# Shorter channel loads, a byte limit on transfers in flight, and a new hand-written order, in a fused RWKV-5 and SwiGLU kernel

## The chip, the cores and the metric

The kernel runs on one core of a Trainium2 chip. A time is the time of one execution on the device, in microseconds (us). Three executions of the kernel before took 593.34, 594.98 and 597.05 us; the median is 594.98 us. One more execution was profiled.

## What is computed

The reference first runs a linear attention with a decaying state (RWKV-5), on 4 batches, 8 heads, 768 tokens and 48 channels a head, and then a SwiGLU layer on the 3072 tokens of 384 features:

```python
for t in range(S):
    kt, vt, rt = (k[:, :, t], v[:, :, t], r[:, :, t])
    cur = np.einsum('bhd,bhe->bhde', u[None] * kt, vt)
    y[:, :, t] = np.einsum('bhd,bhde->bhe', rt, state + cur)
    state = w[None, :, :, None] * state + np.einsum('bhd,bhe->bhde', kt, vt)
...
xn = x / rms * rms_g                  # rms over the 384 features
g = xn @ w_gate                       # 384 x 1536
silu = g * (1.0 / (1.0 + np.exp(-g)))
return ((silu * (xn @ w_val)) @ w_out).astype(np.float32)
```

`w_gate`, `w_val` and `w_out` arrive as 64-bit floats. Everything else is 32-bit.

## The kernel before

**Chunks.** The 768 tokens are cut into 12 chunks `s` of L = 64; a chunk of all 4 batches is NT = 256 tokens. For each chunk SyncE (SP) loads three tiles: `CH` (r and k with channels on the partitions), `TOK` (r and k with tokens on the partitions) and `V`. There is one buffer of each, so a load waits for the last reader of the chunk before. `CH` has 128 partitions: two groups of 64, each with 48 rows of channels and 16 rows of zeros.

**Mixing.** `mixing(s)` does a chunk of attention. For chunks 0 and 1 it multiplies k by u (`ku`, ScalarE), makes the diagonal scores from it (PE products `E`), scales r and k by powers of w (`R`, `K`: VectorE, for half of chunk 0 GpSimd), makes the scores (PE products `A`), puts them behind a mask into `MT` (`d` and `m`, VectorE), and makes the outputs from `MT`, `V` and the state `ST` (PE products `Y`). ScalarE takes `sq` (squares) and `yT` (outputs) out of PSUM; the mean square goes through PE (`r`), VectorE (`ms`), GpSimd (`pow`), VectorE (`inv`, `diag`) and PE (`spread`); `x` is the scaled result, `xb` a copy with the partition halves exchanged. The new state needs `KH` (VectorE, from `TOK` and the table `wk`) and the PE products `U`, which also read `V`. Some outputs are moved to other partitions by two small DMAs (`move`).

**SwiGLU.** The layer of chunks 0 and 1 is done product by product (`cell`, `project`): a product is 12 matmul records. The chunks from 2 on are done in pairs, with seven products in place of eight on sums of weights and of tokens (`group`, `second_layer`). Three PSUM tiles, `bank_a`, `bank_b` and `bank_c`, take the products in turn; `at` is a fourth, for the attention.

**Weights.** Each piece of a weight is loaded as 64-bit words (`raw`, 6 buffers; 384 words a partition for the first six pieces, then 576), and made 32-bit by three engines: `bits` (VectorE, two instructions), `ulp` (ScalarE) and their sum (GpSimd) into `wa`, `wb` or `wo`. In the text "wa0.1" is the second piece of `wa_0`. Later the weights are loaded once more in 36 pieces (`look`), which ScalarE examines (`check`); the result decides whether another version of the whole computation runs. It does not run here.

**Order.** All this is recorded as 1536 steps in a `Plan`. `ORDER` is a list, written out by hand, that says in which order the steps are given; each engine does its own in that order. At the start the numbers mean: 5, 6 loads of k (first and second half of the batches), 7, 8 of r, 9 of `TOK`, 10 of `V`; 11, 16, 21, 26, 31, 36 loads of wa0.0, wb0.0, wa0.1, wb0.1, wa0.2, wb0.2 (each followed by its `ulp`, two `bits` and sum); 41 and 42 `ku`, 43 and 44 `E`, 45 to 48 `R` and `K`, 49 and 50 `A`, 51 and 58 `d`, 52 and 59 `m`, 53 and 60 `Y`, 67 `ms`, 71 `spread`; 100, 101 and 102 the loads of `CH`, `TOK` and `V` for chunk 1.

**Gaps.** Where the plan sees TensorE idle it puts matmuls of a tile of ones with itself (`warm`), one letter of `unused` naming the bank for each gap. They compute nothing.

**Transfers.** Loads on SP go through `InOrder.at_most`: each waits until the fourth load before it has landed (`IN_FLIGHT` = 4). The loads of `look`, the moves and the stores are not counted. SP works in order, so what stands behind a waiting load waits too.

```python
FIRST, IN_FLIGHT = 2, 4
def load_chan(s):
    sp.at_most(IN_FLIGHT, lambda: sp.dma_start(out=CH, in_=chan[s]))
```

Of the kernel before, what the change touches and what calls it, by code (L numbers as in the profile page):

```python
# [49 lines left out]
P = 128  # L50
# [22 lines left out]
def feature_order():  # L73
# [10 lines left out]
    0, 6, 8, 42, 44, 5, 4, 7, 21, 11, 10, 41, 43, 16, 1, 2, 3, 45, 46, 47, 76, 12, 51, 48, 49, 52, 53, 55, 31, 36, 26,  # L84
    13, 14, 58, 50, 59, 15, 54, 17, 22, 60, 62, 65, 66, 100, 18, 19, 23, 24, 113, 9, 108, 103, 20, 67, 68, 83, 56, 27,
    61, 84, 63, 64, 57, 25, 69, 70, 38, 33, 39, 28, 71, 72, 124, 77, 86, 78, 126, 90, 29, 34, 118, 193, 85, 79, 87,
    30, 123, 80, 133, 32, 127, 125, 102, 81, 195, 82, 105, 106, 104, 37, 200, 128, 134, 35, 40, 107, 91, 131, 129,
    109, 114, 95, 130, 132, 92, 135, 119, 73, 110, 136, 96, 137, 155, 115, 111, 120, 116, 205, 210, 121, 139, 140, 97,
    138, 101, 93, 75, 74, 279, 112, 117, 141, 142, 143, 156, 150, 151, 157, 122, 98, 196, 163, 159, 160, 144, 197,
    198, 149, 145, 161, 206, 201, 164, 146, 199, 191, 274, 192, 284, 88, 152, 158, 162, 147, 148, 167, 218, 207, 202,  # L90
    165, 168, 169, 166, 203, 212, 213, 171, 172, 215, 170, 216, 208, 175, 176, 204, 209, 179, 180, 211, 177, 173, 217,
    174, 178, 183, 187, 89, 181, 182, 276, 219, 277, 153, 227, 275, 184, 188, 281, 194, 289, 280, 222, 282, 321, 311,
    306, 185, 225, 189, 247, 248, 249, 186, 214, 154, 190, 99, 278, 283, 251, 252, 255, 285, 250, 253, 254, 220, 256,
    257, 94, 238, 259, 263, 260, 264, 291, 286, 287, 288, 258, 267, 313, 308, 292, 314, 307, 224, 290, 228, 221, 271,
    316, 293, 261, 312, 268, 317, 265, 269, 223, 226, 309, 229, 331, 326, 336, 272, 266, 270, 262, 310, 315, 298, 302,
    294, 295, 242, 230, 322, 233, 234, 328, 355, 352, 318, 323, 299, 303, 296, 231, 300, 304, 297, 232, 353, 356, 235,
    236, 243, 327, 346, 319, 324, 305, 301, 329, 237, 244, 341, 273, 386, 390, 391, 387, 246, 354, 358, 245, 357, 320,
    325, 330, 332, 359, 362, 388, 392, 342, 333, 338, 334, 343, 344, 335, 339, 347, 337, 340, 345, 361, 364, 365, 348,
    360, 389, 375, 407, 349, 380, 363, 383, 381, 239, 393, 384, 500, 350, 366, 406, 394, 395, 351, 368, 369, 416, 437,
    367, 396, 241, 370, 501, 371, 382, 405, 404, 502, 398, 372, 399, 400, 373, 504, 503, 397, 438, 507, 509, 240, 374,  # L100
    376, 408, 378, 512, 377, 401, 402, 445, 409, 410, 385, 403, 413, 439, 446, 456, 457, 417, 441, 440, 447, 411, 442,
    462, 443, 444, 448, 451, 449, 463, 450, 464, 452, 453, 455, 454, 506, 458, 460, 465, 505, 459, 470, 467, 471, 466,
    468, 472, 508, 469, 473, 414, 415, 418, 590, 461, 422, 481, 474, 412, 476, 482, 510, 477, 478, 475, 483, 518, 591,
    513, 480, 484, 489, 485, 511, 479, 486, 490, 491, 487, 514, 488, 628, 492, 627, 519, 515, 520, 525, 493, 495, 624,
    526, 527, 496, 625, 497, 494, 521, 499, 528, 533, 523, 522, 530, 534, 419, 420, 423, 421, 424, 428, 524, 516, 517,
    425, 636, 529, 535, 498, 531, 544, 532, 626, 536, 634, 539, 598, 537, 545, 629, 540, 647, 541, 633, 538, 546, 543,
    547, 552, 635, 549, 548, 542, 550, 551, 630, 553, 631, 555, 554, 558, 632, 556, 563, 559, 560, 562, 565, 564, 557,
    567, 637, 426, 427, 429, 430, 566, 651, 568, 561, 571, 569, 570, 574, 582, 584, 575, 572, 573, 599, 577, 576, 578,
    638, 579, 434, 431, 583, 600, 595, 596, 601, 639, 581, 580, 592, 606, 585, 589, 593, 611, 432, 433, 588, 435, 586,
    602, 603, 587, 597, 436, 607, 642, 612, 643, 700, 640, 594, 747, 644, 701, 608, 615, 645, 756, 641, 652, 609, 610,  # L110
    646, 748, 614, 648, 649, 749, 616, 613, 617, 619, 618, 681, 744, 745, 650, 605, 653, 654, 621, 604, 682, 620, 657,
    746, 622, 683, 623, 660, 826, 689, 656, 684, 655, 685, 754, 690, 757, 753, 751, 691, 686, 706, 687, 688, 692, 695,
    693, 707, 708, 696, 697, 699, 709, 694, 702, 658, 703, 704, 714, 711, 698, 712, 715, 659, 661, 750, 662, 710, 663,
    705, 716, 717, 713, 725, 718, 755, 762, 719, 666, 720, 726, 827, 752, 727, 721, 723, 758, 722, 724, 728, 863, 733,
    860, 730, 664, 665, 763, 734, 729, 731, 732, 667, 669, 735, 736, 759, 760, 739, 864, 737, 769, 740, 771, 861, 741,
    770, 764, 765, 865, 743, 862, 772, 777, 866, 738, 766, 767, 670, 778, 668, 671, 774, 742, 773, 775, 780, 675, 779,
    776, 783, 834, 781, 867, 873, 782, 788, 784, 785, 790, 789, 835, 787, 791, 796, 793, 792, 786, 869, 797, 798, 794,
    795, 799, 802, 883, 800, 870, 676, 807, 803, 804, 806, 809, 808, 810, 801, 815, 812, 672, 673, 674, 677, 816, 768,
    761, 811, 805, 678, 888, 813, 818, 814, 821, 819, 817, 836, 831, 832, 871, 822, 823, 820, 872, 868, 825, 824, 828,
    829, 833, 874, 837, 843, 838, 679, 680, 844, 875, 839, 830, 878, 879, 847, 876, 841, 980, 981, 846, 877, 887, 880,  # L120
    842, 881, 845, 848, 851, 882, 884, 889, 886, 885, 984, 850, 891, 852, 890, 853, 919, 855, 849, 917, 918, 983, 920,
    982, 854, 856, 857, 990, 840, 858, 922, 921, 923, 924, 893, 859, 925, 892, 896, 931, 936, 926, 937, 927, 932, 933,
    928, 942, 929, 935, 944, 943, 945, 986, 938, 985, 939, 894, 930, 940, 934, 993, 895, 947, 950, 998, 987, 951, 946,
    948, 899, 1063, 941, 953, 952, 949, 954, 956, 961, 957, 1096, 958, 963, 962, 960, 964, 988, 992, 955, 965, 966,
    989, 969, 959, 967, 968, 972, 1097, 900, 897, 970, 898, 991, 975, 973, 976, 994, 901, 971, 1098, 905, 1001, 977,
    974, 979, 978, 999, 1005, 1000, 1007, 1006, 1003, 1013, 1008, 1002, 1010, 1009, 1011, 1012, 995, 1102, 1014, 1015,
    1070, 1016, 1019, 1017, 1105, 902, 903, 904, 908, 1062, 1024, 1020, 1021, 1119, 1023, 1026, 1025, 1027, 1018,
    1106, 1028, 1029, 1032, 1022, 1030, 1031, 1035, 1033, 1100, 1034, 1038, 1036, 1043, 1039, 906, 1103, 1040, 1045,
    1044, 1124, 1004, 1037, 909, 907, 911, 996, 1047, 1042, 1046, 1099, 1048, 1041, 1049, 1051, 1071, 1050, 1101,
    1109, 910, 1123, 1054, 1052, 1108, 1104, 1107, 997, 914, 1057, 1055, 1216, 1056, 1110, 1060, 1053, 1058, 1059,  # L130
    1061, 1064, 1072, 1111, 912, 1065, 1114, 1115, 1067, 1068, 1073, 1078, 1074, 1075, 1083, 1172, 1173, 913, 1069,
    1112, 1217, 1066, 1219, 915, 916, 1113, 1116, 1084, 1079, 1117, 1080, 1118, 1120, 1218, 1121, 1122, 1082, 1125,
    1126, 1087, 1229, 1076, 1088, 1086, 1089, 1091, 1085, 1155, 1127, 1153, 1154, 1077, 1128, 1156, 1093, 1094, 1158,
    1157, 1159, 1160, 1220, 1092, 1090, 1081, 1095, 1161, 1167, 1228, 1223, 1162, 1225, 1163, 1164, 1168, 1129, 1169,
    1226, 1165, 1171, 1174, 1221, 1234, 1177, 1299, 1178, 1132, 1180, 1298, 1166, 1222, 1179, 1175, 1176, 1186, 1170,
    1181, 1224, 1227, 1182, 1332, 1183, 1187, 1184, 1185, 1230, 1232, 1130, 1131, 1333, 1188, 1189, 1192, 1190, 1197,
    1193, 1135, 1335, 1194, 1199, 1198, 1235, 1191, 1196, 1200, 1205, 1195, 1202, 1203, 1133, 1134, 1206, 1201, 1138,
    1207, 1208, 1204, 1334, 1211, 1209, 1241, 1212, 1336, 1344, 1231, 1236, 1136, 1213, 1243, 1242, 1210, 1345, 1337,
    1237, 1215, 1244, 1214, 1249, 1238, 1239, 1246, 1245, 1250, 1251, 1247, 1248, 1137, 1139, 1140, 1144, 1252, 1255,
    1253, 1338, 1341, 1254, 1260, 1256, 1257, 1306, 1259, 1262, 1261, 1307, 1263, 1268, 1265, 1258, 1266, 1269, 1264,  # L140
# [18 lines left out]
class InOrder:  # L159


    def __init__(self, tc, engine):
        self.tc, self.engine, self.flying = tc, engine, []

    def at_most(self, n, give):


        made = give()
# [79 lines left out]
def fast(ctx, tc, chan, tok, vpad, wka, wkb, wot, cols, u_row, out, bad):  # L248
# [124 lines left out]
    def load_chan(s):  # L373
        sp.at_most(IN_FLIGHT, lambda: sp.dma_start(out=CH, in_=chan[s]))
# [1477 lines left out]
```

## Time and profile before

| what | value |
|---|---|
| median of three executions | 594.98 us |
| profiled execution | 594.46 us |
| its span, first to last instruction | 592.7 us |
| outside the span | 1.8 us |
| TensorE (PE) busy | 582.0 us, 98% of the span |
| VectorE (DVE), ScalarE (ACT), GpSimd (POOL) busy | 70%, 50%, 7% |
| moved by DMA | 62.99 MB, mean 106 GB/s |
| mean granted TensorE clock | 0.998 |

Busy time is the share of the span in which an engine has an instruction running. PE's matmuls are pipelined and their ends are modelled, so their records overlap: a product of 12 records shows 1.46 us long, but the next starts 1.30 us later. The warm matmuls count as busy. Line 179 is a helper through which nearly all instructions are given, so work is told apart by tiles. "A <- B" in a list of waits means that A was idle until B ended, and "issue" that the profile shows no cause. SPq is SyncE's queue of DMA issues.

### The profile page before, as it was taken

How to read it: one execution, taken by the hardware profiler on the slowest of the kernel's cores; microseconds unless marked ns; L12 is line 12 of the kernel's file. 1: busy time of each engine (PE TensorE's matmuls, PEld its weight loads, DVE VectorE, ACT ScalarE, POOL GpSimd, SP SyncE). 2: the span in 40 equal slices, each digit the busy share in tenths (PEclk: the TensorE clock that was granted, in tenths of full speed). 3: DMA queues.
4: the chain of work that ended last, by engine and by line, in shares of the span. 5: the costliest groups of instructions: out<-in, count | busy, mean ns of one | idle time of the engine just before them, and what ended most of it. 6: DMA issues, size and time to landing. Idle time of an engine off the chain costs nothing.

```text
span 592.7 us, 16598 instructions
## 1 busy us (share of the span) xinstructions
PE 582.0 (98%) x7280; PEld 520.5 (88%) x7280; DVE 415.3 (70%) x622; ACT 293.8 (50%) x713; POOL 41.9 (7%) x40
## 2 busy tenths in 40 slices
PE   8999999999999999999999999999999999999996
PEld 7888887668888998888999889999889999988995
DVE  7888769595786977776795667795777585455641
ACT  5864458364366654564462474584365473124100
POOL 2443234100000000000000000000000000000000
PEclk9999999999999999999999999999999999999999
DMA  7975463412613123512222415301531200301002
GB/s 268 337 254 232 167 239 90 146 34 55 213 55 116 55 75 103 198 36 97 82 92 67 143 58 187 133 8 40 165 119 62 69 29 17 92 2 54 2 4 55
DMA packets 22768, 62.99 MB, mean 106 GB/s; under 512 B 2944, under 2 KB 9760, under 8 KB 21280
## 3 DMA queue, kind: packets, MB, share of 16 engines
q1 hardware_dynamic: 21920, 61.36, 30.8%
q8 instruction: 58, 0.95, 0.7%
q10 hardware_dynamic: 768, 0.49, 0.3%
q14 instruction: 22, 0.18, 0.1%
HBM read 56.04 MB, written 4.72 MB: 103 GB/s over the span
## 4 chain that ended last, share of the span: by engine, by line
PE 95%; DMA 2%; DVE 1%; issue 1%; ACT 0%; SPq 0%; POOL 0%; DVEq 0%
PE bank_b L179 33%; PE bank_c L179 27%; PE bank_a L179 27%; PE at L179 8%; DMA V<-in_vpad_dram 1%; DMA chan<-in_chan_dram 1%; DVE ms L179 0%; DVE KH L179 0%; ACT ku L179 0%; SPq L179 0%; ACT wk L179 0%; POOL ms L179 0%; ACT diag L179 0%; DVE rows_out L179 0%; DVE diag L179 0%
## 5 line engine op out<-in xcount | busy, mean ns | idle before, releaser
L179 DVE TENSOR_TENSOR gv<-bank_b,m 128x512 f32<-128x512 f32 x90 | 62.1, 690 | 63.5 <-PE bank_b L179 59.2
L179 ACT ACTIVATE gv<-gv 128x512 f32<-128x512 f32 (+1 forms) x60 | 30.8, 522 | 74.9 <-DVE gv L179 74.7
L179 DVE TENSOR_TENSOR gv<-bank_c,gv 128x512 f32<-128x512 f32 x60 | 41.4, 690 | 21.7 <-PE bank_c L179 21.2
L179 PE MATMUL bank_b<-xa,wa 64*128 64x256 f32 x444 | 55.3, 379 | 0.0
L179 PEld LDWEIGHTS bank_b<-xa,wa 64*128 64x128 f32 x444 | 43.2, 187 | 5.0 <-issue 0.7
L179 PE MATMUL bank_a<-xb,wb 64*128 64x256 f32 x372 | 46.5, 379 | 0.0
L179 PE MATMUL bank_a<-xa,wa 64*128 64x256 f32 x372 | 46.0, 378 | 0.0
L179 PE MATMUL bank_b<-t,s 64*128 64x256 f32 x360 | 45.2, 379 | 0.6 <-issue 0.6
L179 PE MATMUL bank_a<-wo,h 128*128 128x192 f32 x264 | 45.2, 327 | 0.0
L179 ACT ACTIVATE MT<-dmask,du 128x64 f32<-128x64 f32 x160 | 41.8, 336 | 6.1 <-DVE du L179 6.0
L179 PE MATMUL bank_b<-t,wb 64*128 64x256 f32 x360 | 44.6, 378 | 0.0
L179 PE MATMUL bank_c<-t,s 64*128 64x256 f32 x360 | 44.4, 376 | 0.0
L179 PE MATMUL bank_c<-xb,s 64*128 64x256 f32 x360 | 44.2, 376 | 0.0
L179 PEld LDWEIGHTS bank_a<-wo,h 128*128 128x128 f32 x264 | 43.2, 190 | 0.5
L179 ACT COPY m<-bank_a 128x512 f32<-128x512 f32 (+1 forms) x35 | 19.9, 568 | 47.7 <-PE bank_a L179 39.3
L179 ACT ACTIVATE gv<-bank_a 128x256 f32<-128x256 f32 x30 | 11.5, 382 | 58.6 <-PE bank_a L179 58.6
L179 PEld LDWEIGHTS bank_a<-xb,wb 64*128 64x128 f32 x372 | 36.3, 187 | 4.2 <-issue 0.3
L179 PEld LDWEIGHTS bank_b<-t,s 64*128 64x128 f32 x360 | 35.2, 187 | 5.4 <-issue 1.7
L179 PEld LDWEIGHTS bank_a<-xa,wa 64*128 64x128 f32 x372 | 36.4, 187 | 3.8
L179 ACT ACTIVATE rows_out<-rows_out 128x384 f32<-128x384 f32 x72 | 39.1, 554 | 0.5
L179 PEld LDWEIGHTS bank_c<-t,s 64*128 64x128 f32 x360 | 35.8, 187 | 3.5
L179 PEld LDWEIGHTS bank_c<-xb,s 64*128 64x128 f32 x360 | 35.5, 187 | 3.6
(189 smaller groups left out, 1099.3 us busy)
## 6 DMA issues: line engine op xcount, KB each, us to landing
chan<-in_chan_dram SPq DMA_DIRECT2D x11, 1024.0 KB, 5.4
TOK<-in_tok_dram SPq DMA_DIRECT2D x10, 768.0 KB, 4.7
V<-in_vpad_dram SPq DMA_DIRECT2D x12, 512.0 KB, 5.3
raw<-in_wot_dram SPq DMA_DIRECT2D x8, 576.0 KB, 5.0
rows_out<-in_wka_dram SPq DMA_DIRECT2D x12, 384.0 KB, 3.2
rows_out<-in_wkb_dram SPq DMA_DIRECT2D x12, 384.0 KB, 3.9
rows_out<-in_wot_dram SPq DMA_DIRECT2D x12, 384.0 KB, 3.4
raw<-in_wka_dram SPq DMA_DIRECT2D x6, 576.0 KB, 5.8
```

The lines of the kernel that those rows point to most:

```text
L179: return lambda *args, **kwargs: self.tc.keep_in_program_order(give(*args, **kwargs))
```

## The change

Four things change. From chunk 1 on, `CH` is loaded by two DMAs of 48 partitions each, one for each group; the rows of zeros stay as chunk 0 left them. The limit on transfers in flight is in thousands of bytes (`within`): a load waits for the oldest ones until the sum of those not waited for, itself included, is at most 1800. The `look` loads are counted too, each as 901, so two never fit. `ORDER` is another permutation of the same steps, and `unused` another string.

```diff
 ORDER = [
-    0, 6, 8, 42, 44, 5, 4, 7, 21, 11, 10, 41, 43, 16, 1, 2, 3, 45, 46, 47, 76, 12, 51, 48, 49, 52, 53, 55, 31, 36, 26,
-    13, 14, 58, 50, 59, 15, 54, 17, 22, 60, 62, 65, 66, 100, 18, 19, 23, 24, 113, 9, 108, 103, 20, 67, 68, 83, 56, 27,
-    61, 84, 63, 64, 57, 25, 69, 70, 38, 33, 39, 28, 71, 72, 124, 77, 86, 78, 126, 90, 29, 34, 118, 193, 85, 79, 87,
...
+    0, 5, 8, 6, 7, 41, 42, 43, 44, 4, 11, 10, 21, 1, 2, 47, 3, 46, 45, 16, 12, 76, 26, 49, 51, 52, 48, 50, 53, 13, 14,
+    22, 15, 100, 36, 58, 59, 54, 55, 56, 60, 62, 17, 57, 61, 63, 64, 23, 18, 24, 19, 28, 29, 31, 65, 66, 9, 103, 20,
+    67, 68, 69, 27, 25, 124, 83, 84, 86, 85, 70, 38, 126, 71, 32, 72, 77, 30, 87, 118, 113, 123, 78, 90, 91, 33, 39,
...
-    def at_most(self, n, give):
+    def within(self, limit, size, give):
         made = give()
-        self.flying.append(made.ins)
-        if len(self.flying) > n:
+        self.flying.append((made.ins, size))
+        while len(self.flying) > 1 and sum(x for _, x in self.flying) > limit:
             self.tc.add_manual_dep(
-                made.ins, self.flying.pop(0).name,
+                made.ins, self.flying.pop(0)[0].name,
...
-    FIRST, IN_FLIGHT = 2, 4
+    FIRST, IN_FLIGHT = 2, 1800
...
     def load_chan(s):
-        sp.at_most(IN_FLIGHT, lambda: sp.dma_start(out=CH, in_=chan[s]))
+        for z in range(2):
+            rows = slice(64 * z, 64 * z + D)
+            sp.within(IN_FLIGHT, 393, lambda: sp.dma_start(out=CH[rows], in_=chan[s, rows]))
     def load_tok(s):
-        sp.at_most(IN_FLIGHT, lambda: sp.dma_start(out=TOK, in_=tok[s]))
+        sp.within(IN_FLIGHT, 786, lambda: sp.dma_start(out=TOK, in_=tok[s]))
     def load_v(s):
-        sp.at_most(IN_FLIGHT, lambda: sp.dma_start(out=V, in_=vpad[s]))
+        sp.within(IN_FLIGHT, 524, lambda: sp.dma_start(out=V, in_=vpad[s]))
...
-        p.add("SP", 1.65 * share, [], [r], lambda: sp.at_most(IN_FLIGHT, lambda: sp.dma_start(out=raw, in_=part)), land=LAND, name=f"load {n}")
+        p.add("SP", 1.65 * share, [], [r], lambda: sp.within(IN_FLIGHT, size * P // 125, lambda: sp.dma_start(out=raw, in_=part)), land=LAND, name=f"load {n}")
...
-            "SP", 0.95, [], keys, lambda: sp.dma_start(out=raw, in_=src[:, k * CHECK : (k + 1) * CHECK]), land=3*LAND,
+            "SP", 0.95, [], keys, lambda: sp.within(IN_FLIGHT, IN_FLIGHT // 2 + 1, lambda: sp.dma_start(out=raw, in_=src[:, k * CHECK : (k + 1) * CHECK])), land=3*LAND,
...
-    unused = list("baaaacbbbbbb")
+    unused = list("bbaaccbbbbbbbb")
```

The four quarter loads of chunk 0 go through `within` with 262 each, and the half `TOK` of chunks 0 and 1 with 393.

## The prediction

> **What bounds the kernel.** I read the page's first part, the busy time by stretches, the list of TensorE's waits, the chain that ended last and, for the first 40 us, the timeline of each engine.
>
> The page's busy time, and the stretches of 15 us (columns: length, then busy time with count for PE, PEld, DVE, ACT, POOL, then clock, DMA share and GB/s):
>
> ```profile
> PE 582.0 (98%) x7280; PEld 520.5 (88%) x7280; DVE 415.3 (70%) x622; ACT 293.8 (50%) x713; POOL 41.9 (7%) x40
> ```
>
> ```profile
> 0.00:15.00 15.00, 12.92 (x274) 11.98 (x274) 10.55 (x37) 7.99 (x22) 3.92 (x14) 1.00 0.80 269
> 15.00:30.00 15.00, 13.62 (x298) 12.27 (x300) 13.36 (x23) 12.93 (x32) 6.72 (x7) 1.00 0.96 339
> 30.00:45.00 15.00, 14.26 (x232) 11.90 (x231) 11.80 (x22) 9.71 (x23) 7.44 (x6) 1.00 0.70 257
> 45.00:60.00 15.00, 15.00 (x192) 13.26 (x194) 13.11 (x21) 6.86 (x14) 4.99 (x4) 1.00 0.54 214
> ```
>
> PE is full from 45 us on. Before that the DMA engines are 96% busy from 15 to 30 us, and VectorE and ScalarE nearly full. PE's own waits from 38 us to the end are one line:
>
> ```profile
> PE bank_b L179 <- issue: 0.6, 1, 0.6
> ```
>
> So no wait for data shows in PE's list between 38 us and its last product near 585. The change can win only before that, or lose anywhere. The chain of waits of the first 50 us (start, length, what):
>
> ```profile
> 2.19 4.09 DMA chan<-in_chan_dram
> ...
> 6.30 5.11 DMA V<-in_vpad_dram
> ...
> 11.54 0.91 PE at L179 x48
> ...
> 16.46 0.17 DVE ms L179
> ...
> 19.55 0.71 PE at L179 x2
> ...
> 23.08 1.45 DVE KH L179
> ...
> 24.57 1.15 PE at L179 x64
> ...
> 32.52 1.71 PE at L179 x105
> ```
>
> The first `V` is issued only at 6.30, when the load of k issued at 2.19 has landed, and lands at 11.41; `Y` of the first half waits for it. Then follow the second half, `ms`, `spread` (19.55), `KH`, `U` (24.57) and `Y` of chunk 1, whose first part starts at 31.20. From there PE has no gap but this one of 0.74 us inside `Y`, which no data explains:
>
> ```profile
> 31.20 0.57 PE L179 MATMUL at<-MT,V 64*64 64x64 f32 x23
> 32.52 0.81 PE L179 MATMUL at<-MT,V 64*64 64x64 f32 x41 [0.74 <-issue]
> ```
>
> [...] No large load of this trace covers fewer than 128 partitions, [...]; it shows 339 GB/s over 15 us for full ones. [...] one `bits` instruction takes 0.56 us, and the same beside GpSimd's sum at 14.77 takes 1.25.
>
> ```profile
> 14.06 0.56 DVE L179 SCALAR_TENSOR_TENSOR bits<-raw,bits 128x384 int32<-128x384 int32 x1
> 14.93 1.25 DVE L179 SCALAR_TENSOR_TENSOR bits<-raw,bits 128x384 int32<-128x384 int32 x1
> ```
>
> ```profile
> 14.77 1.00 POOL L179 TENSOR_TENSOR wb<-bits,ulp 128x384 int32<-128x384 int32 x1 [2.38 <-ACT ulp L179]
> ```
>
> **First loads.** Before, the loads of 262 KB landed at about 4.06, 5.1, 6.28 and 7.0 us (ends of the waits of `ku`, `R` and of SP), each freeing one issue. Now wa0.0 goes out at once (4 x 262 + 393 = 1441, under 1800) and `V` after the first landing, near 4.1 instead of 6.3. `V` ends at byte 1965 KB of the queue in place of 2359. By the GB/s of half-microsecond slices, 1965 KB had moved at 8.4 us; landings came 1.0 to 1.65 us after their bytes. So `V` lands at 9.4 to 10.0, not 11.4. It is no longer last.
>
> **Attention of chunk 0.** The order is now k0, r1, k1, r0. `ku` of the first half runs 4.08 to 5.36, of the second 6.3 to 7.5. VectorE has `up` done at 5.25 and puts one `R` and `down` before 6.5, then `K` and the other `R` (0.61 us spacing) until 7.8. PE: `E` at 7.05 and 7.7, `A` at 8.3 to 8.95. Then `d` (7.8 to 8.45) and `m` (9.0 to 9.75; before, to 10.40). GpSimd's `K` needs the second `ku`: 7.55 to 8.82 (1.27). After 3 warm matmuls (0.7 with the switch) the second `A` runs 9.65 to 10.25, now ahead of `Y`. `Y` starts at 10.3 in place of 11.54.
> VectorE: two `bits` (0.9) to 10.6, `d` to 11.3, `m` to 12.0 (before 13.7, since `A` stood behind `Y`). PE: `Y` 0.85, 5 warm (1.15), second `Y` at 12.3 in place of 14.00. From it to the end of `sq` before took 1.47 us, and 0.99 more to `ms`: `ms` could start at 14.7 in place of 16.46.
> Ahead of it on VectorE now stand six `bits` (2.64 us by 0.35 to 0.56 each) from 12.0: 14.65; but two wait for wb0.0 and wb0.1, bytes up to 2752 and 3145 KB, landing near 12.2 and 13.4, and GpSimd's sum can lock one for 0.7. So 14.7 to 15.4. GpSimd has to end its sum first: `pow` at 15.5 in place of 16.70. From `pow` to `spread` 2.85: `spread` at 18.4, 1.2 earlier.
>
> **Chunk 1.** Its two `CH` loads wait for the second `A` (10.25) and go out at 10.3 in place of 13.11; they end at byte 3931 KB and land near 15.1 at 339 GB/s. ScalarE reaches them at 17.0. After `spread`: `rms` at 19.2 (0.4), `ku` 1.28, `wk` 1.07, `KH` at 22.1 (0.95 to 1.45), `U` at 23.2 in place of 24.57.
> Meanwhile VectorE does `R`, one `gv` and four `bits`: 18.4 + 3.6 = 22.0, so both arrive together. Then `bits` of wa1.0 (1.15), `K` to 25.3, `d` to 26.6, `m` to 28.0 or, with locks and `A` on PE (`E` 1.35 plus a gap of 0.65 as before, `A` to 27.3), to 28.7 (before 30.9).
> `V` of chunk 1 goes out when `U` ends, 24.3 in place of 25.80; at the median 5.3 us it lands at 29.4, without traffic ahead at 27.5. PE by then has also done the second half of `wb` for bank_b, a product (1.5 us) that before stood after `A`. So `Y` starts at 28.8 to 29.4 in place of 31.20: 1.8 to 2.4 earlier, and I take 2.2. After `Y` the products left are the same.
>
> **The rest.** Products, stores and the last 30 us are the same steps. In the recorded orders I count PE's changes between kinds of tiles after that `Y`: 70 before, 71 after; the first product after one takes 1.50 in place of 1.29, so +0.2. Nine warm matmuls fewer: only filling, counted above.
> Half-height `CH` loads: 786 KB take 2.3 us at 339 GB/s, [...] against 3.1 for the old 1049. Price -0.8 to +0.9 of transfer a chunk. Later it is hidden: between its release and its first reader stand 14 us or more of products. Chunk 1 has 1.9 us before ScalarE asks, but wa0.2 behind it would be 0.7 late for ScalarE; I take 0.2, inside the 2.2.
> A byte limit lets three 590 KB pieces fly in place of four: 1.77 MB or 5.2 us of traffic, which still fills the queue. Cost nothing.
> A `look` waits for the one before, 3.2 to 3.9 us from issue to landing; behind it on SP stand moves, stores and loads. The shortest cover I find after 40 us, adding up the products between a load's release and its reader, is 7.6 us (`V` of chunk 10, between `U` and `Y`); a `V` load takes 5.3. So 2.3 us of waiting is free there, and 5 or more elsewhere. Cost 0, bounds 0 and +5.
>
> **Sum.** -2.2 + 0.2 + 0 = -2.0. The profiled execution took 594.46: 592.5. It lies 0.5 under the median of the three runs; from that it would be 593.0. I say 592.7.
>
> **Rivals.** (a) The start gains nothing: `ms` stands behind `bits` that wait for wb0.1, and if it lands 2 us later the old 16.46 is back; or `CH` at half rate makes `ku` late. For: DMA is 96% busy there. Against: its bytes come 400 KB earlier. 594.7.
> (b) Slower: SP stands at a `look` while the one before lands, and `V` of chunk 10 behind it comes late. It decides from 2.3 us of waiting; a whole landing (3.9) plus a transfer before it (4.7 for `TOK`) costs 6.3, and 592.7 + 6.3 = 599.0. Against: the look there is issued 8 us of products before `V` is free.
> (c) More: the gaps of 0.65 and 0.74 marked "issue" vanish; `A` ends at 26.6, `m` at 28.0, and `Y` starts there, 1.0 earlier than my 29.0, and is 0.74 shorter: another 1.7, 591.0. For: no data stands behind them. Against: short matmuls under full DMA will be there again.
>
> **Numbers.** Forecast 0.60 (591.5 to 594.2); (a) 0.18, (b) 0.12, (c) 0.10. The range, 590.0 to 596.4, leaves out most of (b) and the far end of (c). 1%, about what a measurement of this kernel can tell from no change, is 5.9 us: to win that PE would have to lose six of the 14.4 us that it lacks real products before 38.8 us (I add these, each kind at its spacing in the timeline, to 24.4), and 6.4 of the 14.4 are over before the first load is used. Faster 0.06, same 0.87, slower 0.07.
>
> **What would show it.** After: `V` no longer in the chain, first `Y` near 10.3, `ms` near 15, `spread` near 18.4, `Y` of chunk 1 near 29, PE full from there and no wait over 0.6 after 38 us; two `CH` issues a chunk. Wrong if `Y` of chunk 1 starts later than 30.5 or before 27.5, or if PE shows waits of microseconds on `at` behind DMA.

## The result: 0.8% slower

The changed kernel takes 600.57 us (median of 7 executions, 597.83 to 601.28), the kernel before 595.71 (7 executions, 593.34 to 597.43). The ratio is 1.0082, 95% interval 1.0058 to 1.0107. The forecast was 592.7 with a range up to 596.4. The profiled execution took 601.02 us, 6.56 more than that of before.

The page after, busy time, and the two lines that changed most: the first DMA queue (packets, MB, share of 16 engines) and the channel loads (KB each, median us to landing).

```profile
PE 583.4 (97%) x7262; PEld 519.8 (87%) x7262; DVE 415.7 (69%) x622; ACT 294.5 (49%) x713; POOL 41.1 (7%) x40
```

```profile
q1 hardware_dynamic: 21744, 58.48, 34.6%
...
chan<-in_chan_dram SPq DMA_DIRECT2D x22, 384.0 KB, 6.5
```

Before, that queue moved 61.36 MB in 30.8% of the engines' time, and a load of 1024 KB landed after 5.4 us. Now fewer bytes take more engine time, and a load of 384 KB needs longer than one of 1024 KB did (the second of a pair lands behind the first: of the two issued from 153.35, 6.5 us after its issue against 4.4). TensorE's busy time is about the same (583.4 and 582.0 us) while the span grew from 592.7 to 599.3, so most of the loss is waiting. A part of it goes with TensorE's granted clock: of the seven executions, the four with a mean clock of 0.989 or 0.990 took 600.57 us or more, the three with 0.993 to 0.998 took 597.83 to 599.24.

The same stretches of 15 us as in the prediction:

```profile
0.00:15.00 15.00, 11.85 (x213) 11.21 (x214) 10.70 (x37) 7.06 (x19) 4.25 (x13) 0.77 0.75 231
15.00:30.00 15.00, 12.66 (x275) 10.91 (x274) 10.76 (x20) 10.77 (x30) 6.31 (x6) 1.00 0.90 270
30.00:45.00 15.00, 12.33 (x259) 11.29 (x261) 12.77 (x22) 8.64 (x15) 6.36 (x5) 0.89 0.93 242
45.00:60.00 15.00, 15.00 (x188) 13.06 (x187) 12.00 (x19) 8.38 (x20) 2.77 (x2) 1.00 0.57 191
```

From 15 to 45 us the DMA engines are together busier than before (0.90 and 0.93 against 0.96 and 0.70), yet they move (270 + 242) x 15 us = 7.7 MB in place of 8.9. And the clock column, 1.00 in all four before, is 0.77 and 0.89 in two.

The chain of waits of the first 45 us, in which `V` of chunk 0 no longer stands, but the loads do:

```profile
1.25 4.06 DMA chan<-in_chan_dram
...
7.43 1.13 PE bank_c L179 x32
...
14.34 8.72 DMA raw<-in_wka_dram
...
23.14 0.54 ACT ulp L179
...
26.24 1.60 DVE KH L179
...
27.89 1.21 PE at L179 x61
29.11 5.04 DMA V<-in_vpad_dram
...
34.29 2.06 PE at L179 x128
...
42.07 2.91 PE bank_b L179 x12
```

The first quarter of k lands at 5.31 us (before, at 4.0; here it is the other half of k that is loaded first). wa0.2, issued behind the two halves of `CH`, needs 8.72 us and lands at 23.06; ScalarE, which works in order, stands at its `ulp`, and `diag`, `ku`, `wk` and `KH` behind it are late. `Y` of chunk 1 starts at 34.29 in place of 31.20. The line at 42.07 is a product whose record is 2.93 us long where others are 1.46: it follows a gap of 1.03 us, and the granted clock is 0.50 to 0.54 from 41.5 to 45.0, which makes the 0.89 of that stretch.

TensorE's waits from 38 us to the end, one line before:

```profile
PE bank_b L179 <- issue: 1.6, 1, 1.6
PE bank_b L179 <- POOL ms L179: 1.0, 1, 1.0
PE bank_b L179 <- DVE gv L179: 0.4, 1, 0.4
```

The 1.6 us come while SP's eleventh and last `CH` load, that of chunk 11, is under way, beside `Y` of chunk 10 (the expectations below call it the load of chunk 10). "issue" says that the profile shows no cause, but VectorE's and TensorE's own timelines put one beside it: VectorE stands with the channel load and gives its sums late. (That this is the cause is argued here; the run with the looks not counted, below, supports it.)

```profile
441.49 1.22 DVE L179 TENSOR_TENSOR RR<-chan,up 128x1024 f32<-128x1024 f32 x1 [1.18 <-DMA chan<-in_chan_dram]
```

```profile
442.85 1.24 PE L179 MATMUL bank_b<-t,s 64*128 64x256 f32 x9 [1.55 <-issue]
```

The 0.4 us on `gv` show who else pays. At 154.62 a `TOK` goes out right behind two halves of `CH`, takes 7.39 us (the median is 4.6), and VectorE stands for it:

```profile
154.62 7.39 DMA TOK<-in_tok_dram
```

```profile
162.03 0.96 DVE L179 TENSOR_TENSOR TOK<-TOK 128x768 f32<-128x768 f32 x1 [1.35 <-DMA TOK<-in_tok_dram]
```

### The profile page after: what moved, and what is told of

It reads as the page before. It is cut to its first block, busy times and chain, and to the rows that moved or that the text cites. A ratio compares the mean times of both kernels' runs of the same rounds, so it can differ in the third digit from the quotient of the medians.

```text
span 599.3 us, 16572 instructions
## 1 busy us (share of the span) xinstructions
PE 583.4 (97%) x7262; PEld 519.8 (87%) x7262; DVE 415.7 (69%) x622; ACT 294.5 (49%) x713; POOL 41.1 (7%) x40
## 3 DMA queue, kind: packets, MB, share of 16 engines
q1 hardware_dynamic: 21744, 58.48, 34.6%
## 4 chain that ended last, share of the span: by engine, by line
PE 92%; DMA 4%; DVE 1%; ACT 1%; issue 0%; SPq 0%; POOL 0%; DVEq 0%; ACTq 0%; POOLq 0%
PE bank_b L179 32%; PE bank_c L179 26%; PE bank_a L179 26%; PE at L179 8%; DMA raw<-in_wka_dram 1%; DMA TOK<-in_tok_dram 1%; DMA V<-in_vpad_dram 1%; DMA chan<-in_chan_dram 1%; ACT ku L179 1%; SPq L179 0%; DVE KH L179 0%; ACT wk L179 0%; POOL wa L179 0%; DVE TOK L179 0%; DVE bits L179 0%
## 5 line engine op out<-in xcount | busy, mean ns | idle before, releaser
L179 ACT ACTIVATE gv<-gv 128x256 f32<-128x256 f32 (+1 forms) x60 | 31.1, 521 | 72.9 <-DVE gv L179 72.5
L179 PEld LDWEIGHTS bank_b<-t,wb 64*128 64x128 f32 x360 | 34.9, 187 | 3.9
```

The lines of the kernel that those rows point to most:

```text
L179: return lambda *args, **kwargs: self.tc.keep_in_program_order(give(*args, **kwargs))
```

## The experiments

Three theories at the outset: H, the half-height loads are slow and hold the queue; B, the limit in bytes costs, at the start or through the looks; O, the order alone. Ratios below are to the kernel before, run on the same chip, with 95% intervals.

### One part alone, or one part undone

**The old order in the changed kernel.**

```diff
-ORDER = [0, 5, 8, 6, 7, ...        unused = list("bbaaccbbbbbbbb")
+ORDER = [0, 6, 8, 42, 44, ...      unused = list("baaaacbbbbbb")
```

> The changed kernel with the list ORDER and the string unused of the kernel before; the half-height loads and the byte limit stay. Three theories of the 4.9 us that the change lost (medians 595.7 and 600.6): H, the half-height channel loads move slowly and hold back the queue in the first 45 us and chunk 10; B, the byte limit lets a fifth load out beside the four quarters, the first k lands at 5.3 instead of 4.1 us and TensorE loses time and clock; O, the new order alone. O: about 595.7. H: about 600, with CH of chunk 1 landing late and a wait behind it. B: 598 to 600, with the first ku again at 5.3 or later. I lean to a mixture, 598.

598.09 us, 1.0047 (1.0029 to 1.0066). Still slower without the new order: O isn't the cause by itself. But B's account of the start fails: the fifth load goes out at 3.14 us here too, and the first `ku` starts on time.

```profile
4.02 1.28 ACT L179 ACTIVATE ku<-chan,col 128x128 f32<-128x128 f32 x4 [1.73 <-DMA chan<-in_chan_dram]
```

**Whole channel loads in the changed kernel, limit 1800.**

```diff
-        for z in range(2):
-            rows = slice(64 * z, 64 * z + D)
-            sp.within(IN_FLIGHT, 393, lambda: sp.dma_start(out=CH[rows], in_=chan[s, rows]))
+        sp.within(IN_FLIGHT, 1049, lambda: sp.dma_start(out=CH, in_=chan[s]))
```

> The changed kernel with CH of each chunk loaded in one DMA of all 128 rows (1049 thousand bytes in the limit). H: most of the loss is gone, 596 to 597, the stretches of 15 to 45 us move well over the 270 and 242 GB/s of the changed kernel, wa0.2 lands before 21 us (23.06 with the halves), and the wait of 1.55 us at 441 us is gone. B and O: still 600 to 601, since the first gap at 5.44 us and the orders on GpSimd and VectorE are the same. I lean to 597.5.

598.26, 1.0071 (1.0040 to 1.0102). Taken alone this spoke against H. But the trace had a new wait: `TOK` was issued at 154.56, when the `CH` issued at 149.83 had landed, because 1049 + 786 is over 1800; VectorE stood 3.45 us for it, TensorE 2.48 at 162.8. The edit had brought a cost of its own. It is repeated below with room for both.

**Half-height loads alone in the kernel before.**

```diff
-        sp.at_most(IN_FLIGHT, lambda: sp.dma_start(out=CH, in_=chan[s]))
+        for z in range(2):
+            rows = slice(64 * z, 64 * z + D)
+            sp.at_most(IN_FLIGHT, lambda: sp.dma_start(out=CH[rows], in_=chan[s, rows]))
```

> The kernel before with nothing but the two loads of 48 rows per chunk (both counted in the limit of four). H: slower by 2 to 5 us, 597.7 to 600.7, with under 300 GB/s from 15 to 45 us. B and O: 595.7 or up to 1 us less, since fewer bytes are moved. I lean to 598.

599.68, 1.0062 (1.0030 to 1.0093). H by itself makes a loss of this size, in the old order and without any limit in bytes. In the profiled execution (605.19 us, the slowest of nine) the stretch from 15 to 30 us moved 280 GB/s in place of 339, and `Y` of chunk 1 came at 35.8.

**The new order alone in the kernel before.**

> The kernel before with the new list ORDER and the new string unused alone: whole loads of CH, four transfers in flight. O: about 600. H and B: 594 to 596; if the prediction's account of the order was right by itself, with the fifth load held back, Y of chunk 1 comes 1 to 2 us earlier than 31.20 and the time is 593.5 to 594.7. I lean to 596.

595.52, 1.0000 (0.9979 to 1.0022); the edit is the reverse of the first one. The order by itself neither costs nor gains: `Y` of chunk 1 at 32.7, not earlier than the old 31.2. It is this order, with the fifth load still held back, that makes the first k late:

```profile
5.07 2.56 ACT L179 ACTIVATE ku<-chan,col 128x128 f32<-128x128 f32 x8 [2.77 <-DMA chan<-in_chan_dram]
```

**Whole loads again, with room in the limit.**

```diff
-    FIRST, IN_FLIGHT = 2, 1800
+    FIRST, IN_FLIGHT = 2, 1900
+        sp.within(IN_FLIGHT, 1049, lambda: sp.dma_start(out=CH, in_=chan[s]))
```

> The changed kernel with CH loaded whole (1049) and the limit raised from 1800 to 1900, so that CH and TOK (1835 together) fit, which they did not in the earlier whole-CH run; looks are counted as 951, still one at a time. If half height is all of the loss and the earlier run's 2.5 us wait at 162 us came from TOK standing at the limit: 595 to 596, without that wait. If the limit in bytes costs by itself: 597 to 598.5. I lean to 595.8.

596.42, 1.0010 (0.9995 to 1.0026). With everything else of the change in place, but for the 1900, whole loads take the time back to that of the kernel before. Its stretches from 15 to 45 us:

```profile
15.00:30.00 15.00, 12.55 (x291) 10.96 (x287) 12.97 (x22) 12.00 (x31) 7.09 (x7) 1.00 0.88 319
30.00:45.00 15.00, 14.40 (x236) 12.12 (x230) 12.37 (x21) 9.23 (x18) 5.71 (x6) 1.00 0.88 298
```

319 and 298 GB/s at a share of 0.88, where the halves gave 270 and 242 at 0.90 and 0.93. By the timelines, `Y` of chunk 1 starts at 31.6 (with halves 34.3), of chunk 2 at 77.7 (82.0), of chunk 10 at 429.7 (434.7), of chunk 11 at 477.6 (484.7). These two traces are further apart than the kernels: the profiled executions took 593.96 and 601.02 us, the medians differ by 4.2.

**Halves only from chunk 3 on.**

```diff
+        if s < 3:
+            sp.within(IN_FLIGHT, 1049, lambda: sp.dma_start(out=CH, in_=chan[s]))
+            return
```

> The changed kernel with CH of chunks 1 and 2 loaded whole and half-height loads from chunk 3 on; limit 1900, new order. By the traces of the changed kernel and of the one with whole CH, Y of chunk 1 was 2.7 us apart, Y of chunk 2 4.3, Y of chunks 4 to 10 about 5, Y of chunk 11 7.1 us. So if the start is most of it, 596.4 plus 1 to 2.5: 597.5 to 599, with the wait at chunk 10 in it. If the later loads are all of it: 600. If the start is all: 596.4.

599.48, 1.0067 (1.0044 to 1.0091), 3.1 us above the whole loads by the medians, with nothing else changed. So the later loads are enough for most of the loss, which I hadn't expected: the traces alone put more of it at the start. Whether the first two add to it is not clear of noise (1.0067 against 1.0082). The trace shows two late places, VectorE waiting 1.8 us for `TOK` at 161 us, and 1.6 for `TOK` and 1.5 for `CH` between 400 and 450, and with each place goes 0.8 us of wait for TensorE. This trace also lost time in its first 13 us, where nothing differs from the kernel above; that is taken up below.

### What a half-height load does

**Two loads of full height.** Is it that two loads take two of the four places in flight?

```diff
+        for z in range(2):
+            sp.at_most(IN_FLIGHT, lambda: sp.dma_start(out=CH[:, z], in_=chan[s, :, z]))
```

> The kernel before with CH of chunks 1 on loaded by two DMAs of all 128 rows, r and k apart (524 thousand bytes each, both counted among the four in flight). Rival C of theory H: two loads where one was take up two of the four places in flight, and that is what cost the half-height kernel its 3.7 us: 598 to 600 here too. H: 595.3, at most 0.7 more, with slices near 400 GB/s.

595.65, 1.0006 (0.9985 to 1.0026). Two loads cost nothing when both have 128 rows. So it is not the number of loads; what is left is the height (a row has 4 KB here and 8 KB in the halves).

**Rows 0 to 111 in one load,** in the kernel before and in the changed one.

```diff
+        rows = slice(0, 64 + D)
+        sp.at_most(IN_FLIGHT, lambda: sp.dma_start(out=CH[rows], in_=chan[s, rows]))
```

> The kernel before with CH of chunks 1 on loaded by one DMA of rows 0 to 111 (918 thousand bytes; the last 16 rows of zeros stay). Theory H says that it is the half height of one DMA that is slow: rows 0 to 111 then move near the 385 to 418 GB/s that whole CH loads show in slices of 1 us, take 2.3 us in place of 2.7, and the time is 595.3 or up to 0.7 less. Rival N: every load that leaves rows out is slow, 150 GB/s in its slices, and the time 598 or more.

> The changed kernel with CH of chunks 1 on loaded by one DMA of rows 0 to 111, counted as 918 (with TOK 1704, under the limit of 1800); new order, limit in bytes and counted looks stay. If half height is all of the loss: 595 to 596. If the limit in bytes costs by itself, at the looks (each holds CH back until TOK has landed) or at the first k (landing at 5.3), 597 to 599. I lean to 596.5.

597.37, 1.0037 (1.0020 to 1.0055), and 597.18, 1.0035 (1.0020 to 1.0049). Leaving out 16 rows saved nothing and cost some 2 us: neither what H nor what its rival said. In the slices of 1 us (columns as in the prediction, the last two DMA share and GB/s) these loads showed 311 to 369 GB/s, so 131 thousand bytes less took about the same time. Where the 2 us go is not shown. From the changed kernel with 112 rows:

```profile
388.72:389.72 1.00, 1.00 (x8) 1.00 (x7) 1.00 (x1) 0.74 (x3) 0.00 (x0) 1.00 1.05 369
389.72:390.72 1.00, 1.00 (x8) 1.00 (x7) 1.00 (x2) 0.44 (x2) 0.00 (x0) 1.00 1.05 311
```

**64 rows a load.**

```diff
+            rows = slice(64 * z, 64 * z + 64)
```

> The kernel before with CH of chunks 1 on loaded by two DMAs of 64 rows each (0 to 63, 64 to 127), zeros included, 524 thousand bytes each. Theory P (the rate goes with the rows): slices of 200 to 215 GB/s, the pair takes 5 us as with 48 rows, since each row still has 8 KB to take, and the time is that of the 48-row kernel, 598 to 600. Rival E (a half-height load has one rate): slices near 150, the pair takes 7 us, 601 or more.

601.88, 1.0113 (1.0092 to 1.0135). The rates are P's, or a little over; the time is in the range that E named, so it does not decide between them, and why it is longer than with 48 rows is open. Slices of 1 us of single loads. First a whole one in the kernel before, issued at 102.14:

```profile
103.10:104.10 1.00, 1.00 (x5) 0.60 (x4) 1.00 (x3) 0.98 (x5) 1.00 (x1) 1.00 0.70 139
104.10:105.10 1.00, 1.00 (x5) 0.60 (x4) 1.00 (x1) 0.97 (x2) 1.00 (x2) 1.00 0.98 410
105.10:106.10 1.00, 1.00 (x5) 0.60 (x4) 0.77 (x2) 0.06 (x1) 1.00 (x1) 1.00 1.07 451
```

Two of 48 rows in the changed kernel, issued from 153.35:

```profile
155.40:156.40 1.00, 1.00 (x14) 0.89 (x12) 0.59 (x2) 0.98 (x3) 0.00 (x0) 1.00 1.05 148
156.40:157.40 1.00, 1.00 (x12) 0.90 (x10) 0.40 (x1) 1.00 (x5) 0.00 (x0) 1.00 0.99 172
157.40:158.40 1.00, 1.00 (x12) 0.90 (x10) 1.00 (x2) 0.59 (x3) 0.00 (x0) 1.00 1.03 145
```

Two of 64 rows, issued from 308.57:

```profile
310.57:311.57 1.00, 1.00 (x8) 1.00 (x7) 1.00 (x2) 0.85 (x2) 0.00 (x0) 1.00 1.02 238
311.57:312.57 1.00, 1.00 (x9) 1.00 (x8) 1.00 (x1) 0.00 (x0) 0.00 (x0) 1.00 0.98 238
312.57:313.57 1.00, 1.00 (x8) 1.00 (x8) 0.97 (x2) 0.00 (x0) 0.00 (x0) 1.00 1.05 238
```

All the full slices show a share near 1 (0.98 to 1.07): the engines are taken up either way, and move a third or a half (145 to 172 and 238 against 410 to 451 GB/s). At 150 GB/s two halves of 393 KB take 5.2 us; at 415 one whole of 1049 KB takes 2.5 (estimates from the slices' rates).

**Rows from the middle.** The rate could go with the number of rows (theory P), or with where they lie (theory W).

```diff
+        for lo, hi in ((32, 96), (0, 32), (96, 128)):
+            sp.at_most(IN_FLIGHT, lambda: sp.dma_start(out=CH[lo:hi], in_=chan[s, lo:hi]))
```

> The kernel before with CH of chunks 6 to 11 loaded by three DMAs: rows 32 to 95 (524 thousand bytes), then 0 to 31, then 96 to 127 (262 each); chunks 1 to 5 whole. Theory W (ways): [...] that load runs near the whole load's 385 to 451 GB/s and takes 1.2 to 1.3 us, and the other two, [...] near 210 for 1.2 us each: some 3.7 us in all [...]. Theory P (rows alone): the first near 215 GB/s for 2.4 us, the others near 108, 7.3 us in all. Time: W 595 to 597, P 598 or more.

596.60, 1.0029 (1.0009 to 1.0049), in W's range and still above the kernel before. Slices of half a microsecond, chunk 8, issued from 303.98:

```profile
305.98:306.48 0.50, 0.50 (x5) 0.50 (x4) 0.50 (x2) 0.50 (x1) 0.00 (x0) 1.00 0.95 377
306.48:306.98 0.50, 0.50 (x5) 0.50 (x4) 0.50 (x1) 0.35 (x2) 0.00 (x0) 1.00 0.97 410
306.98:307.48 0.50, 0.50 (x6) 0.50 (x5) 0.50 (x1) 0.00 (x0) 0.00 (x0) 1.00 1.28 393
307.48:307.98 0.50, 0.50 (x5) 0.50 (x5) 0.50 (x1) 0.00 (x0) 0.00 (x0) 1.00 0.97 197
307.98:308.48 0.50, 0.50 (x5) 0.50 (x5) 0.47 (x2) 0.00 (x0) 0.00 (x0) 1.00 0.82 213
```

64 rows from the middle move at 377 to 410 GB/s, and the 32 rows at each end at 197 to 214. The same number of rows taken from 0 to 63 gave 196 to 238. So the number of rows doesn't decide alone: the rates are near those that theory W named, and where the rows lie counts. What ties a row's place to a rate is not shown. Most full slices show 135 to 172 GB/s for loads of 48 rows, 196 to 238 for 64, 311 to 369 for 112 and 385 to 451 for 128. In the middle of these ranges the four loads take 2.6, 2.4, 2.7 and 2.5 us (estimates: 393, 524, 918 and 1049 thousand bytes at 153, 217, 340 and 418 GB/s). So by these rates leaving rows out in these ways shortened no single load by more than 0.1 us, which would tell why the 112 rows gain nothing.

**Two queues.**

```diff
+            rows, by = slice(64 * z, 64 * z + D), (sp, pool)[z]
+            sp.at_most(IN_FLIGHT, lambda: by.dma_start(out=CH[rows], in_=chan[s, rows]))
```

> The kernel before with CH of chunks 6 to 11 loaded by two half-height DMAs, the second of which is issued by GpSimd on another queue; chunks 1 to 5 stay whole. This asks what limits a half-height load to 135 to 172 GB/s. Theory P, [...] a load's rate goes with its rows (48 of 128 rows: 0.375 of about 415, 156): both halves moving at once give near 300 GB/s and land within 1 us or so of each other. Rival E, the DMA engines or the queue are slow with such a load: together still about 150 to 170 GB/s. Time: P 595 to 597, E 597 to 600.

603.47, 1.0133 (1.0102 to 1.0165), above both ranges. Inconclusive: only in chunks 6 and 10 were the halves issued together with no other large load; there the slices show 128 to 258 GB/s, between the two expectations, with small transfers among them. In chunk 11 they went out 0.8 us apart, beside a `TOK`; the other three pairs moved apart, since GpSimd issued its half 10.9 to 39.4 us earlier.

### The limit in bytes and the start

**The looks not counted.**

```diff
-            "SP", 0.95, [], keys, lambda: sp.within(IN_FLIGHT, IN_FLIGHT // 2 + 1, lambda: sp.dma_start(out=raw, ...)), ...
+            "SP", 0.95, [], keys, lambda: sp.dma_start(out=raw, ...), ...
```

> The changed kernel with the look loads not counted in the limit; half-height loads, bytes and order stay. Theory L: the counted look before CH of chunk 10 makes that load wait until TOK has landed, 5.7 us after TOK's issue (1.4 us in the kernel before), and the wait of 1.55 us at 441 us comes from it: 598 to 599, without that wait. If the half height alone is late there, or nothing of the loss is there: 600 to 601.

600.72, 1.0100 (1.0066 to 1.0134): no gain. The wait at that last `CH` did go, though. In the changed kernel SP had issued there

```profile
428.25 0.33 SPq L179 DMA_DIRECT2D TOK<-in_tok_dram  x1
431.29 0.33 SPq L179 DMA_DIRECT2D rows_out<-in_wot_dram  x1
433.97 0.80 SPq L179 DMA_DIRECT2D chan<-in_chan_dram  x2
```

with the halves 5.7 us after `TOK`, when it had landed; with the looks free they went out 1.2 us after it (430.25), `R` ran at 441.71 without a wait, and TensorE had no gap there. Instead VectorE waits 2.34 for `TOK`, which now shares the queue with the halves, and TensorE 0.6 at 438.2.

**The limit in bytes alone in the kernel before (1900, whole loads),** with the looks counted and without.

> The kernel before (its order, whole CH) with the limit in bytes alone, 1900 and each look 951. Theory B, the limit costs by letting a fifth load out beside the first four: 597 to 599. Without B: 594.5 to 596.

> The kernel before with the limit in bytes (1900), whole CH, and the looks not counted. If the 1.7 us that the limit cost in this order come from the looks one at a time: 595 to 596. If they come from the bytes (TOK of chunk 2 held back by pieces of 604 in flight, issued at 82.9 us in place of 79.1): still 596.5 to 597.5. I lean to the latter, 596.8.

597.14, 1.0036 (1.0020 to 1.0051), and 598.50, 1.0079 (1.0051 to 1.0108). In the old order the limit costs 1.7 to 3.5 us and the looks aren't the reason; in the new order, whole loads and limit together gave 1.0010. A `TOK` goes out at 82.88 in place of 79.06, as expected (by count of loads it is that of chunk 3, and a piece of a weight is 590 thousand bytes, not 604); but the lost time in these two traces stands in gaps marked "issue", at different places. Why the limit costs in one order and not in the other stays open. With the halves, in the old order, the limit costs nothing that shows (1.0047 against 1.0062 without it).

**The first gap.** The changed kernel waits 2.00 us before `E`, and its short products then take 1.13 us for 32 records in place of 0.69. The two kernels with whole loads in chunks 1 and 2 (all whole; halves from chunk 3 on) are the same program up to there, and their traces part at that gap. All whole:

```profile
1.15 4.78 PE L179 MATMUL bank_b<-ones 128*128 128x128 f32 x24 [1.15 <-DVE h L179]
7.56 0.69 PE L179 MATMUL bank_c<-chan,ku 48*64 48x64 f32 x32 [1.63 <-ACT ku L179]
```

Halves from chunk 3 on:

```profile
1.15 4.31 PE L179 MATMUL bank_b<-ones 128*128 128x128 f32 x24 [1.15 <-DVE h L179]
7.51 1.13 PE L179 MATMUL bank_c<-chan,ku 48*64 48x64 f32 x32 [2.05 <-ACT ku L179]
```

`E` starts at the same time, but after a gap of 2.05 in place of 1.63 it runs at the slow rate, and by the first `Y` it is 1.5 us behind (13.5 against 12.0), by `Y` of chunk 1 1.9 (33.5 against 31.6). The gap is longer because the same 24 filling records took 4.31 us in place of 4.78: the two executions differed in TensorE's rate before it. And the length of a gap doesn't decide. With halves and the fifth load held back (below), the rate falls within `A`, after 0.36 and 1.33 us:

```profile
6.76 0.69 PE L179 MATMUL bank_c<-chan,ku 48*64 48x64 f32 x32 [0.36 <-ACT ku L179]
...
9.26 1.03 PE L179 MATMUL at<-RR,chan 48*64 48x64 f32 x32 [1.33 <-DVE RR L179]
```

The kernel before with the new order alone slows in the same place after 0.50 and 1.31. All whole, which waits 1.63 and then 1.29, keeps the full rate. The granted clock shows the slow rate as a half: in the changed kernel it is 1.00 up to 7.4 us, 0.50 from there to 14.0 and 1.00 again from 14.5. The slow rate came here after gaps of 1.3 to 2.1 us, and after gaps of 1.29 and 1.63 it did not come; what decides is not shown.

**A longer first filling,** and **the fifth load held back** (quarters counted as 378 with whole loads, 355 with halves).

```diff
-            for _ in range(4 * int((until + 0.4 - 3.75) / 0.86)):
+            for _ in range(4 * int((until + 0.4 - 3.75) / 0.86) + 8):
```

> The changed kernel with 8 more warm matmuls in the first filling (32 in place of 24), which reach from 5.4 to about 6.9 us and cover most of the gap of 2.0 us before E. If TensorE's drop to half clock after that gap is part of the loss: first Y at 11.5 to 12 in place of 12.69, and 598.5 to 600 in the end. If not (the loads set the pace anyway): 600 to 601. I lean to 600.2.

604.92, 1.0166 (1.0128 to 1.0204), from 600.80 to 612.19 over six executions; without the longest the median is 603.99. The filling overshot: a warm matmul leaves two records, so it grew from 24 records to 40 and lasted until about 8.7 us, and `E` started at 8.66, later than the 7.43 of the changed kernel. Then no short product ran slow, and the first `Y` came at 11.6. But the time got worse, and the one profiled was the fastest. The time follows the granted clock, from 600.80 us at 0.996 to 612.19 at 0.981; where the others lost it is not seen.

```diff
-                            IN_FLIGHT, 262, lambda: sp.dma_start(out=CH[:, i, half], in_=chan[s, :, i, half])
+                            IN_FLIGHT, 378, lambda: sp.dma_start(out=CH[:, i, half], in_=chan[s, :, i, half])
```

> The new order and limit of 1900 with whole CH, and the four quarter loads counted as 378 in place of 262, so that wa0.0 waits for the first of them and V for the second. If the late first k (5.3 us) and its gap before E were costing: k lands at 4.1, E starts by 6.5 with no gap over 0.6, Y of chunk 1 at 30 to 31, and the time is 594 to 595.3, perhaps below the kernel before. If V, now issued later, takes the gain back: 595.5 to 596.5, as with whole CH alone (596.4).

> The changed kernel with the four quarter loads counted as 355 (limit 1800), which holds wa0.0 and V back in the same way; the half-height loads stay. If the first gap and the clock are 2 us of the loss: 598.3 to 599, Y of chunk 1 at 32 to 33 in place of 34.3. If the half-height load behind it sets the pace whatever comes before: 600 to 601, Y of chunk 1 at 33.5 or later.

596.18, 1.0023 (1.0008 to 1.0038), and 599.17, 1.0075 (1.0055 to 1.0095). The first k landed at 4.80 and 4.55, not at 4.1. With halves the first gap fell to 0.36 us and `Y` of chunk 1 came at 33.2 in place of 34.3, but the first `Y` at 12.70, no earlier than the 12.69 of the changed kernel. The median is 1.4 lower, the ratio only 1.0075 against 1.0082, so at most a microsecond or so was gained, and that is not clear of noise. With whole loads nothing was gained. No version tried beats the kernel before; the new order alone, the two full-height loads, and whole loads in the changed kernel with 1900 equal it.

## Why the prediction was wrong

**The half-height load** is the step that failed. It was priced at "-0.8 to +0.9 of transfer a chunk", and then "I take 0.2, inside the 2.2". The +0.9 was my estimate, which no load in the trace before could show, and it was too small. By the rates above a pair costs about 5.2 - 2.5 = 2.7 us of the engines' time more than one whole load. By the pages it is somewhat less: that queue was busy for 207 us after (34.6% of 599.3), 183 before and 190 in the run with whole loads and 1900, so 1.6 to 2.3 us for each of 11 pairs. Of these 17 to 25 us some 4 reach the total: adding the halves to the kernel before costs 4.4 us (599.68 - 595.28), taking them out of the changed one saves 4.2 (600.57 - 596.42). The effects don't simply add up, though:

| order | limit | whole `CH` | half-height `CH` |
|---|---|---|---|
| old | four loads | 1 | 1.0062 |
| old | in bytes | 1.0036 | 1.0047 |
| new | four loads | 1.0000 | not run |
| new | in bytes | 1.0010 | 1.0082 |

(The limit in bytes is 1900 for whole loads, 1800 for halves.) With the limit in bytes the halves cost 0.7% in the new order and 0.1%, which is not clear of noise, in the old one. So what a slow load costs in the end seems to depend on what the order puts behind it. Which part of the order that is has not been shown, and the new order with halves under the limit of four was not measured.

**"Later it is hidden"** failed too. The cover of 14 us was counted for the `CH` load alone. What comes late is what shares the queue: `TOK`, and wa0.2 at the start ("0.7 late for ScalarE"; it was 1.54 us, and `diag` and `ku` stood behind it). At the last `CH` the limit moved its issue to 5.7 us after `TOK` (1.4 before), so the cover itself shrank. Cost 0 became about 3 us by the run with late halves (1.0067 against 1.0010).

**The landings of the first loads** were kept as before. The first k came at 5.3, not 4.1. The fifth load let out beside them is not the cause that it seemed: in the three runs with the old order and that load out early the first `ku` starts at 4.02 to 4.08; in all ten with the new order, which loads the other half of k first, it starts at 4.55 to 5.49, with the fifth load or without. Why that half lands later is open. `V` indeed left the chain, but `E` stood at 7.43 and ran at a granted clock of 0.50 (1.13 us for 32 records in place of 0.69), a cost no step had: each gap that the sum left in TensorE was priced at its own length. First `Y`: 10.3 expected, 12.69 measured.

**VectorE before the first `A`** was mis-priced too. With the new order alone `E` starts at 7.10, near the 7.05 expected, but `A` at 9.58 and the first `Y` at 12.94. `A` waits 1.31 us for the second `R`, which takes 1.78 us in place of 0.68 beside GpSimd's `K`:

```profile
7.75 1.78 DVE L179 TENSOR_TENSOR RR<-chan,up 128x512 f32<-128x512 f32 x1
```

```profile
7.71 1.27 POOL L179 TENSOR_TENSOR chan<-chan,down 128x512 f32<-128x512 f32 x1 [5.45 <-ACT ku L179]
```

Five traces with the new order show this (1.76 to 1.80). The prediction had shown the same for `bits` (1.25 us beside GpSimd's sum, 0.56 without), and had this `K` start at 7.55, before the `R` ended, but counted 0.61 for the `R`.

**`CH` of chunk 1** went out at 13.02, not 10.3, as it waits for that same `A`. `Y` of chunk 1 at 34.3 is past the 30.5 that the text had named as its limit.

**The order's -2.0** isn't there: alone it measures 1.0000, with `Y` of chunk 1 at 32.7, by the two steps above and, in that trace, the slow rate from `A` on.

**The looks at cost 0:** right for the time (600.72 without the count), but not because they delay nothing: counted they make `CH` late, not counted `TOK` comes late. Rival (b) had SP standing at the limit in the right place, but the load that came late is `CH`, not `V`, and the wait 1.55 us in place of 6.3. Rival (a) named "`CH` at half rate makes `ku` late", but ended at 594.7, as if a slower load could only take back a gain. None of the cases had the half rate as a loss of its own.

## What to carry to other kernels

Price a DMA by where its rows lie before its bytes: leaving out rows of zeros in this way saved 25% of the bytes and about doubled the engines' time (5.2 against 2.5 us, estimates from the slices' rates), and 64 rows moved at 377 to 410 GB/s from rows 32 to 95 and at 196 to 238 from rows 0 to 63. When a transfer gets slower, ask who stands behind it in the same queue, not only who reads it. And when undoing one edit under a limit, make sure that what you put back fits the limit, or the experiment tests the limit.

## What the hardware showed that I had not expected

- A load of 64 rows moved at 377 to 410 GB/s from rows 32 to 95 and at 196 to 238 from rows 0 to 63; one of 112 rows moved at 311 to 369 where one of 128 moved at 385 to 451, about as long a load by these rates (2.7 and 2.5 us, estimates).
- In two kernels that are the same program up to there, TensorE's records ran at 0.69 us for 32 in one execution and at 1.13 in the other. Gaps of 1.31, 1.33 and 2.05 us were followed by the slow rate, gaps of 1.29 and 1.63 in another trace were not.
- With the old order, which loads one half of k first, the first `ku` started at 3.95 to 4.18 us in ten traces; with the new one, which loads the other half first, at 4.55 to 5.49 in ten. Why is open.
